# Two waves of an attention and MLP kernel: token order in the copies of x, and one store per output block

## The chip, the cores and the metric

The kernel runs on one core of a Trainium2 chip. The metric is the device time of one execution in microseconds (us); lower is better. Engines are called as the profile does: PE is TensorE (PEld its weight loads), DVE is VectorE, ACT is ScalarE, POOL is GpSimd, SP is SyncE, which here only issues DMAs. A q behind the name (SPq) is the engine's own instruction queue.

## The reference

Inputs are q, k and v of 4 batches, 8 heads, 768 positions and 64 dimensions, a decay `lam` per head, and two weights. A causal attention with decay runs in blocks of 64 positions with a state that is carried on; its output is turned into 3072 tokens of 512 channels, and an MLP follows:

```python
intra = np.einsum('bhic,bhjc->bhij', qb, kb) * Dmask[None]
intra = np.einsum('bhij,bhjd->bhid', intra, vb)
inter = np.einsum('bhid,bhde->bhie', qb * lam_pow[None], kv_state)
out[:, :, sl] = intra + inter
kv_state = lam_block[None, :, None, None] * kv_state + np.einsum('bhsd,bhse->bhde', kb_dec, vb)
...
h = x @ w_in                                  # 512 -> 2048
g = h * (1.0 / (1.0 + np.exp(-1.702 * h)))    # GELU, sigmoid form
return (g @ w_out).astype(np.float32)         # 2048 -> 512
```

Every token's output depends on its own x alone in the MLP, so tokens may stand in any order there as long as the store puts them back.

## The kernel before, in words

The work goes in six waves of 512 tokens. Waves 0 and 1 (`w < ND`) take the first 256 positions of two batches each: batch 2w+c for c = 0, 1. Waves 2 to 5 take 128 positions of all four batches. Within a wave the attention part makes xT[w], a bf16 tile of 128 partitions (channels) by 4 rows r of 512 columns (tokens). `mlp1`, `mlp1_half` and `in_product` then multiply it by w_in, GELU goes to g_sb, and `product0` (wave 0) and `product` (the others) multiply g_sb by w_out. The two products are made mostly by a seven-product scheme on halves: PE works on halves of 256 tokens and of the channels, and DVE forms the sums (`x_sums`, `g_sums`, `weight_sums`).

**Order of tokens in the first two waves.** q, k and v are loaded with `"h (s a) d -> s h (a d)", a=2`: partition s holds positions 2s and 2s+1. So the attention output of 128 positions comes out of PE with its 128 columns as (a s): first the 64 even positions, then the 64 odd ones. `d_x` (L328) copies such a PSUM bank `[128, 4, 128]` into 128 adjacent columns of each of the four rows of xT. It is called four times a wave, for c = 0, 1 and i = 0, 1, with columns from (2c+i)*128: five of the eight copies go to ACT (L224, `act_copy`), three to DVE (L221, `dve_copy`): the last of each `end(w, c)`. All columns of the MLP keep the order (a s), and so does the output block: partition p = 64a+s holds position 2s+a. Stores undo it: each block of 128 partitions by 2x256 f32 is stored in two transfers of 64 partitions (`A` and `Z`) into every second row of out, by `store` in `leave0` (L537, wave 0, kept in `late` and issued later by hand) and by `after_product` (L492, wave 1). Waves 2 to 5 store 128 partitions at once (L496).

**Order of the work.** Instructions stand on each engine's queue in the order in which the kernel is written (`manual_schedule`); a layer beneath puts the waits in, from what each instruction reads and writes. The places that matter:

- Wave 0, its last copies: `end(0, 1)` (L765), with `d_x` for i = 0 on ACT and i = 1 on DVE. Then three `mlp1_half` (L767): the first on the columns of c = 0, the next two on c = 1; then `mlp1` for 12 pieces of w_in, `in_sums`, `sums` and `weight_sums` on DVE, and `product0`.
- Wave 1: `end(1, 0)` (L822), `mlp1_half(1, 0, 14, 15)`, more attention, `a1 b1 a2` (`in_product` on columns of c = 0), `end(1, 1)` (L837), `x_sums(1, (0,))`, then "b2" (L839, `in_product` n = 2: rows 2 and 3 of xT, columns of c = 0), then `mlp1_half(1, 1, 14, 15)` (L842) on columns of c = 1.
- SP's queue: loads of wave 2, `late[2]`, `late[5]` (L846), transposes of wave 2 by DMA (L248), loads of v, `late[3]`, `late[4]`, loads of wave 3, the stores of wave 1, the transposes of wave 3, and so on. A DMA takes one of eight semaphores in turn.

Of the kernel before, what the change touches and what calls it, by code (L numbers as in the profile page):

```python
# [25 lines left out]
def kernel(  # L26
# [13 lines left out]
    nc = tc.nc  # L40
    f32 = mybir.dt.float32
    bf16 = mybir.dt.bfloat16
    B, H, S, D = q.shape
    P = 128
# [70 lines left out]
    A, Z = slice(0, 64), slice(64, P)  # L115
# [78 lines left out]
    cast, trans, masked, xT, g_of, h_ps, o_ps, t_ps = {}, {}, {}, {}, {}, {}, {}, {}  # L194
# [132 lines left out]

    def d_x(w, c, i, t, copy):  # L328
        n0 = (2 * c + i) * P
        copy(xT[w][:, :, n0 : n0 + P], t)  # L330

    def n_scores(w, p):
        s2 = [acc("ps_s") for _ in range(2)]
# [117 lines left out]
    def product(w, n, ts):  # L451
        last = w == NW - 1
        key = ts[0] if last else 0
        if n == 1 and (last or ts[0] == 0):
            for c in "QVX":
                blocks[w, c, key] = acc(f"ps_{c}", shape=[P, 2, 256], tag="a" if last and ts[0] else "mm")
        bank = blocks[w, CHAIN[n], key]
        sums, raw = half_sum.get(w, [None] * 4), [[token_half(w, i, kh) for kh in range(2)] for i in range(2)]
        x = {1: raw[0][0], 2: raw[0][1], 4: raw[1][1], 5: sums[0], 6: sums[1], 7: sums[2], 3: sums[3]}[n]
        for t in ts:  # L460
            for m in range(FFC // 2):
                y = {1: (0, 0), 2: (1, 0), 3: (1, 1)}.get(n)
                y = w_half(m, *y) if y else TS[{4: 3, 5: 0, 6: 1, 7: 2}[n]][:, m]
                nc.tensor.matmul(bank[:, t], x[:, m, t * P : (t + 1) * P], y,  # L464
                                 start=(n in (1, 2, 7) and t == ts[0] * last and m == 0),
                                 stop=(m == FFC // 2 - 1), skip_group_check=True)
        if last or ts[-1] == 1:
            t = slice(ts[0], ts[0] + 1) if last else slice(0, 2)
            if n == 2 and 0 < w < NW - 1:
                c11[w] = partial(after_product, w, n, bank, t)  # L470
            else:
                after_product(w, n, bank, t)

    def after_product(w, n, bank, t):
        if n in (1, 6, 7):
            part[w, n, t.start] = op.tile([P, 2, 256], f32, tag="part", bufs=6, name="part")
            nc.scalar.copy(part[w, n, t.start][:, t], bank[:, t])
            if (w, 4, t.start) in c12:
                after_product(w, 4, c12.pop((w, 4, t.start)), t)
            return  # L480
        if n == 4 and (w, 6, t.start) not in part:
            c12[w, 4, t.start] = bank
            return
        o = op.tile([P, 2, 256], f32, tag="o", name="o_sb")
        if n == 3:
            nc.scalar.copy(o[:, t], bank[:, t])
        else:
            nc.vector.tensor_tensor(o[:, t], part[w, {2: 1, 5: 7, 4: 6}[n], t.start][:, t], bank[:, t], op=ADD)
        i, c = {2: (0, 0), 3: (0, 1), 4: (1, 0), 5: (1, 1)}[n]
        cols = slice(256 * c, 256 * c + 256)  # L490
        if w < ND:
            rows5 = out.rearrange("(b t s a) d -> a b s t d", t=S // P, s=64, a=2)  # L492
            for a, rows in enumerate((A, Z)):
                nc.sync.dma_start(out=rows5[a, 2 * w + i, :, 0:2, cols], in_=o[rows])
        else:
            nc.sync.dma_start(  # L496
                out=out.rearrange("(b s) d -> s b d", s=S)[w * P : (w + 1) * P, 2 * i + t.start : 2 * i + t.stop, cols],
                in_=o[:, t])
# [19 lines left out]
    def leave0(n):  # L518
        bank = blocks[0, BANK0[int(n)]]
        if n in (1, 6, 7):  # L520
            part[0, n] = op.tile([P, 2, 256], f32, tag="part", bufs=6, name="part")
            nc.scalar.copy(part[0, n], bank)
            return
        if n == 4.5:
            nc.gpsimd.tensor_tensor(o21[0], o21[0], part[0, 7], op=ADD)
            return
        o = op.tile([P, 2, 256], f32, tag="o", name="o_sb")
        if n == 3:
            nc.scalar.copy(o, bank)
        else:  # L530
            nc.vector.tensor_tensor(o, part[0, {2: 1, 5: 7, 4: 6}[n]], bank, op=ADD)
        if n == 4:
            o21.append(o)
        i, c = {2: (0, 0), 3: (0, 1), 4: (1, 0), 5: (1, 1)}[n]

        def store():
            rows5 = out.rearrange("(b t s a) d -> a b s t d", t=S // P, s=64, a=2)  # L537
            for a, rows in enumerate((A, Z)):
                nc.sync.dma_start(out=rows5[a, i, :, 0:2, 256 * c : 256 * c + 256], in_=o[rows])
        late[n] = store  # L540

    GR = {w: (1, 2, 0, 3) if w > 1 else (1, 2, 3) for w in range(1, NW)}
# [144 lines left out]
    with tc.manual_schedule():  # L687
# [31 lines left out]
        do_cast(0, 1, "q", nc.vector, 0)  # L719
        do_cast(0, 1, "q", nc.vector, 1)  # L720
        d_x(0, 0, 0, oa, act_copy)
        turn_pe(0, 1, "q", act_copy, 0)
        d_inter(0, 0, oz, 0, False)
        turn_pe(0, 1, "k", dve_copy, 1)
        turn_pe(0, 1, "q", dve_copy, 1)
        d_x(0, 0, 1, oz, act_copy)
        fill(1, "a")
        d_scores(0, 1, 0, True)
# [19 lines left out]
        def end(w, c):  # L748
            oa, oz = d_out(w, c)
            t = acc("ps_kv", shape=[P, NP, D]) if w else states[w, c]  # L750
            if w == 0:
                nc.scalar.copy(seen, oz[:, 3, P - 1 : P])
            d_state(w, c, t, Z)
            if w == 0:
                d_inter(w, c, oz, 0, False)
            d_x(w, c, 0, oa, act_copy)
            d_x(w, c, 1, oz, dve_copy)
            if w == 0:
                nc.scalar.copy(kv_sb[0][:, 2 * w + c], t)
            return partial(nc.vector.tensor_tensor, kv_sb[0][:, 2 * w + c], kept.get((w, c)), t, op=ADD)  # L760
# [131 lines left out]
```

## Time and profile before

| what | value |
|---|---|
| runs | 193.22 us median of 3 (192.25, 193.22, 193.78) |
| profiled execution | 193.47 us, its span 191.8 us |
| granted clock of PE | 1.0 |
| copies into xT, waves 0 and 1 | 5 on ACT, mean 591 ns; 3 on DVE, mean 691 ns |
| copies into xT, later waves (L397) | 16 on ACT, mean 600 ns |
| stores of 64 partitions, 128 KB (L494, L539) | 16, issue 605 and 606 ns of SP (median) |
| stores of 128 partitions, 256 KB (L496) | 12 |
| DMA traffic | 33.91 MB, 177 GB/s over the span |

The span goes from the first to the last instruction that the profile shows; the execution's time is 1.67 us longer. A line of the timeline has the start in us, the length in us, the engine, the line of the kernel, the operation, the tile written and those read, and how many such instructions are merged; in square brackets stands the idle time before it and what ended it. A group's line ends with the sum of busy time in us, the mean of one in ns, and the idle time ahead of the group's instructions. Matmuls are pipelined: one may be shown as 272 ns while the next starts 109 ns later.

### The profile page before, as it was taken

The page shows a single profiled execution, that of the slowest core. Times are in us where ns is not written, and L with a number is a line of the kernel's source. Part 1 is how long each engine was busy: PE and PEld are TensorE (multiplying, and loading weights), DVE is VectorE, ACT ScalarE, POOL GpSimd, SP SyncE. Part 2 cuts the span into 40 slices and gives each one's busy share as a digit, 9 for nine tenths or more (in the row PEclk, how much of TensorE's full clock was granted, in tenths as well). Part 3 has the DMA queues.
Part 4 walks back from the last instruction along what each step waited for, and adds up shares of the span by engine and source line. Part 5 has one row for each costly group of instructions (what it writes and reads, how often), then busy time and mean ns, then how long its engine had stood idle before and what let it go on. Part 6 is the DMA issues. An engine that isn't in the chain of part 4 may idle for free.

```text
span 191.8 us, 5553 instructions
## 1 busy us (share of the span) xinstructions
PE 183.5 (96%) x2291; PEld 150.7 (79%) x2293; DVE 154.6 (81%) x296; ACT 130.0 (68%) x243; POOL 53.8 (28%) x79
## 2 busy tenths in 40 slices
PE   7779999999999999999999999999999999999993
PEld 2356545898788888888888888888888888888882
DVE  1797689997687899979799879799889797889950
ACT  4858566055869976389878388877388876597711
POOL 5298200029738000096000294000393000000000
PEclk9999999999999999999999999999999999999999
DMA  5999999999996799988899756999365903300113
GB/s 154 322 241 161 199 206 206 277 291 295 258 174 139 162 228 243 241 206 135 190 244 221 228 137 140 226 249 251 104 163 121 208 4 113 109 3 0 53 57 112
DMA packets 89599, 33.91 MB, mean 177 GB/s; under 512 B 67430, under 2 KB 89446, under 8 KB 89574
## 3 DMA queue, kind: packets, MB, share of 16 engines
q1 hardware_dynamic: 84676, 28.84, 61.7%
q0 software_dynamic: 4896, 4.72, 14.9%
q8 instruction: 18, 0.29, 0.7%
q14 instruction: 7, 0.06, 0.1%
q10 hardware_dynamic: 2, 0.00, 0.0%
HBM read 27.26 MB, written 6.29 MB: 175 GB/s over the span
## 4 chain that ended last, share of the span: by engine, by line
PE 79%; DMA 12%; DVE 4%; POOL 2%; SPq 1%; issue 0%; ACT 0%; ACTq 0%
PE ps_X L464 19%; PE ps_hX L596 17%; PE ps_V L464 9%; PE ps_hV L596 9%; DMA w_out<-in_moe_w_out_dram 6%; DMA vf<-in_v_dram 6%; PE ps_Q L464 5%; PE ps_hQ L596 4%; PE ps_X L514 3%; DVE w_out_t L431 2%; PE ps_s L338 2%; PE ps_o L393 2%; PE ps_h L417 2%; DVE g_s L444 2%; POOL w_in L184 1%; PE ps_o L380 1%
## 5 line engine op out<-in xcount | busy, mean ns | idle before, releaser
L615 ACT ACTIVATE g_sb<-h_sb 128x512 bf16<-128x512 f32 x57 | 34.5, 632 | 1.2 <-DVE h_sb L604 1.2
L464 PEld LDWEIGHTS <-g_s 128*128 128x128 bf16 x320 | 30.9, 98 | 4.1
L596 PEld LDWEIGHTS <-w_in_t 128*128 128x128 bf16 x304 | 29.7, 98 | 3.6
L224 ACT COPY part<-ps_hX 128x512 f32<-128x512 f32 x34 | 19.5, 586 | 10.4 <-PE ps_hX L596 10.3
L464 PEld LDWEIGHTS <-g_sb 128*128 128x128 bf16 x240 | 22.8, 98 | 3.4
L596 PEld LDWEIGHTS <-w_in 128*128 128x128 bf16 x228 | 22.1, 98 | 2.8
L596 PE MATMUL ps_hX<-x_s,w_in_t 128*128 128x256 bf16 x152 | 22.5, 272 | 0.0
L444 DVE TENSOR_TENSOR g_s<-g_sb 128x1024 bf16<-128x1024 bf16 (+1 forms) x26 | 16.5, 646 | 5.5 <-ACT g_sb L615 5.5
L464 PE MATMUL ps_X<-w_out_t,g_s 128*128 128x256 bf16 x160 | 19.1, 273 | 0.0
L682 POOL CAST behind_q<-x_s 1x1 f32<-1x1 bf16 x4 | 0.7, 174 | 62.2 <-DVE x_s L577 62.2
L212 POOL TENSOR_TENSOR qs<-qf,q_pow 128x512 bf16<-128x512 f32 x16 | 16.3, 1040 | 0.9 <-PE ps_o L301 0.9
L212 POOL TENSOR_TENSOR ks<-kf,k_pow 128x512 bf16<-128x512 f32 x16 | 16.3, 1039 | 0.1
L604 DVE TENSOR_TENSOR h_sb<-part,ps_hX 128x512 f32<-128x512 f32 x19 | 12.9, 681 | 3.9 <-PE ps_hX L596 3.9
L221 DVE COPY part<-ps_hV 128x512 f32<-128x512 f32 x18 | 12.4, 687 | 3.2 <-PE ps_hV L596 3.2
L604 DVE TENSOR_TENSOR h_sb<-part,ps_hV 128x512 f32<-128x512 f32 x19 | 13.0, 684 | 1.0 <-PE ps_hV L596 1.0
L604 DVE TENSOR_TENSOR h_sb<-part,ps_hQ 128x512 f32<-128x512 f32 x19 | 12.9, 681 | 0.4 <-PE ps_hQ L596 0.4
L615 ACT ACTIVATE g_sb<-ps_hX 128x512 bf16<-128x512 f32 x19 | 11.1, 588 | 1.9 <-PE ps_hX L596 1.9
L347 ACT ACTIVATE sm<-ps_s,inv_pow 128x512 bf16<-128x512 f32 x16 | 10.2, 691 | 2.5 <-PE ps_s L338 2.5
L224 ACT CAST v_sb<-vf 128x1024 bf16<-128x1024 f32 (+1 forms) x12 | 10.4, 906 | 1.6 <-DMA vf<-in_v_dram 1.6
L596 PE MATMUL ps_hQ<-xT,w_in 128*128 128x256 bf16 x76 | 11.4, 273 | 0.0
L596 PE MATMUL ps_hV<-x_s,w_in_t 128*128 128x256 bf16 x76 | 11.4, 273 | 0.0
L596 PE MATMUL ps_hV<-xT,w_in_t 128*128 128x256 bf16 x76 | 11.4, 273 | 0.0
(128 smaller groups left out, 364.4 us busy)
## 6 DMA issues: line engine op xcount, KB each, us to landing
kf<-in_k_dram SPq DMA_DIRECT2D x10, 512.0 KB, 6.3
qf<-in_q_dram SPq DMA_DIRECT2D x10, 512.0 KB, 6.7
vf<-in_v_dram SPq DMA_DIRECT2D x10, 512.0 KB, 5.9
out_dram<-o_sb SPq DMA_DIRECT2D x24, 128.0 KB, 2.4
out_dram<-o_sb SPq DMA_DIRECT2D x12, 256.0 KB, 2.6
w_out<-in_moe_w_out_dram POOLq DMA_DIRECT2D x4, 512.0 KB, 14.8
kf<-in_k_dram SPq DMA_DIRECT2D x4, 256.0 KB, 3.1
qf<-in_q_dram SPq DMA_DIRECT2D x4, 256.0 KB, 4.6
```

The costliest lines, as they stand in the source:

```text
L212: eng.tensor_tensor(x.rearrange("p b (r i j d) -> p j (b r) i d", i=2, j=2, d=D)[:, j], f.rearrange("p h (a d) -> p (h a) d", a=2).rearran ...
L221: nc.vector.tensor_copy(out, in_)
L224: nc.scalar.copy(out, in_)
L338: nc.tensor.matmul(s2[h][:, b, :], kT[hs, (b % 2) * NP + p, :], qT[hs, (b % 2) * NP + p, :], start=True, stop=True)
L347: nc.scalar.activation(sm, s, COPY, scale=inv_pow[:, n : n + 1])
L393: nc.tensor.matmul(ps_o[cs, b, :], vt[:, b, 2 * p + i, :], masked[w, 2 * R + i, j][:, b, :], start=False, stop=True, skip_group_check=True)
L444: nc.vector.tensor_tensor(o, x, y, op=f)
L464: nc.tensor.matmul(bank[:, t], x[:, m, t * P : (t + 1) * P], y, start=(n in (1, 2, 7) and t == ts[0] * last and m == 0), stop=(m == FFC // ...
L514: nc.tensor.matmul(bank[:, t], x[:, m, t * P : (t + 1) * P], y, start=(n in (1, 2, 7, 4) and t == 0 and m == 0), stop=(m == FFC // 2 - 1), ...
L596: nc.tensor.matmul(bank[:, u], z[:, kc], y[:, kc], start=(n in (1, 2, 7) and u + kc == 0), stop=(kc == 1), skip_group_check=True)
L604: nc.vector.tensor_tensor(h, h_part[w, g, {2: 1, 5: 7, 4: 6}[n]], bank, op=ADD)
L615: nc.scalar.activation(g_of[w][:, a : b + 1 : b - a, 256 * i : 256 * i + 256], bank, GELU)
```

## The change

In `d_x` the copy writes with a step of two elements: the columns of PSUM, (a s), go to columns (s a) of xT, so that tokens stand in natural order from there on. Each output block of waves 0 and 1 then holds 128 successive positions, and one transfer of 128 partitions stores it.

```diff
     def d_x(w, c, i, t, copy):
         n0 = (2 * c + i) * P
-        copy(xT[w][:, :, n0 : n0 + P], t)
+        copy(xT[w][:, :, n0 : n0 + P].rearrange("p r (s a) -> p r a s", a=2), t.rearrange("p r (a s) -> p r a s", a=2))
...
         if w < ND:
-            rows5 = out.rearrange("(b t s a) d -> a b s t d", t=S // P, s=64, a=2)
-            for a, rows in enumerate((A, Z)):
-                nc.sync.dma_start(out=rows5[a, 2 * w + i, :, 0:2, cols], in_=o[rows])
+            nc.sync.dma_start(out=out.rearrange("(b t s) d -> b s t d", t=S // P, s=P)[2 * w + i, :, 0:2, cols], in_=o)
...
         def store():
-            rows5 = out.rearrange("(b t s a) d -> a b s t d", t=S // P, s=64, a=2)
-            for a, rows in enumerate((A, Z)):
-                nc.sync.dma_start(out=rows5[a, i, :, 0:2, 256 * c : 256 * c + 256], in_=o[rows])
+            nc.sync.dma_start(out=out.rearrange("(b t s) d -> b s t d", t=S // P, s=P)[i, :, 0:2, 256 * c : 256 * c + 256], in_=o)
```

Lines behind L492 have numbers two lower in the changed kernel, those behind L537 four lower.

## The prediction

> **What bounds the kernel now.** I read the page's busy shares first, then the chain that ended last, then the timeline round the eight copies, and last what each engine waited for.
>
> ```profile
> PE 183.5 (96%) x2291; PEld 150.7 (79%) x2293; DVE 154.6 (81%) x296; ACT 130.0 (68%) x243; POOL 53.8 (28%) x79
> ...
> PE 79%; DMA 12%; DVE 4%; POOL 2%; SPq 1%; issue 0%; ACT 0%; ACTq 0%
> ```
>
> TensorE holds the chain for 79% of the span. In order of time that chain is a DMA of w_out until 29.07 us, vector work (L431, L444) until 37.20, and from 37.24 to 188.6 TensorE alone. So what makes TensorE later after 37.24 is paid in full, and what makes it later before can be lost in its waits for DMA and for L431. The share of the page is too coarse for a change of this size; the two stretches with the last copies of each wave decide. First the timeline of wave 0:
>
> ```profile
> 18.50 2.79 PE L417 MATMUL ps_h<-xT,w_in 128*128 128x256 bf16 x24
> 18.56 0.69 DVE L221 CAST xT<-ps_o 128x512 bf16<-128x512 f32 x1 [1.37 <-PE ps_o L301]
> ...
> 21.14 1.03 PE L405 MATMUL ps_h<-xT,w_in 128*128 128x512 bf16 x3
> ...
> 22.51 9.67 PE L405 MATMUL ps_h<-xT,w_in 128*128 128x512 bf16 x44 [0.35 <-DMA w_in<-in_moe_w_in_dram]
> ...
> 36.38 0.60 PE L514 MATMUL ps_V<-w_out_t,g_s 128*128 128x256 bf16 x4
> ...
> 37.24 0.60 PE L514 MATMUL ps_W<-w_out_t,g_sb 128*128 128x256 bf16 x4 [0.26 <-DVE w_out_t L431]
> ```
>
> The reader is to see that L417 starts at 18.50 while VectorE's copy of the wave's last 128 tokens still runs until 19.25, and that TensorE later waits twice, for w_in (22.51) and for L431 (37.24). The same place in wave 1:
>
> ```profile
> 54.35 0.69 DVE L221 CAST xT<-ps_o 128x512 bf16<-128x512 f32 x1
> 54.49 0.61 PE L596 MATMUL ps_hQ<-xT,w_in 128*128 128x256 bf16 x4
> 55.01 1.37 SPq L248 DMA_TRANSPOSE kT<-ks  x1
> 55.09 0.77 PEld L417 LDWEIGHTS <-w_in 128*128 128x128 bf16 x8 [0.27 <-DVE xT L221]
> 55.10 1.05 PE L417 MATMUL ps_h<-xT,w_in 128*128 128x256 bf16 x8
> ```
>
> Four matmuls of L596 run beside the copy, and L417 waits for its end (55.04). They fill TensorE's wait.
>
> **Part 1: the waits of TensorE.** In the built program no instruction of PE, DVE, ACT or POOL is added, removed or moved. Two waits of PE move, and no other wait between compute engines does. In both waves the wait for the last x copies (VectorE's and ScalarE's) stood ahead of the first matmul on the second 256 tokens; now it stands ahead of one that reads only the first 256. In wave 0 it moves from the first matmul of the c=1 half at L767 to the second one of the c=0 half: the first of that half reads row 0 of xT, columns 0 to 255, which lie ahead of the written ones, and does not wait. In wave 1 it moves from the half at L842 to the four matmuls of "b2" (L839). It looks as if the layer that sets waits takes a strided write as one stretch from its first to its last element, rows between included.
>
> *Wave 1.* "b2" starts after the copy, at 55.09 and not at 54.49, and L417 behind it. Eight matmuls of 128x256 start 0.87 us apart (32.02 to 32.89, L514), so one takes 0.109 us and four 0.44. L417 starts at 55.53, not 55.10: **+0.44 us**. Queued behind it on TensorE is everything up to 188.6, a chain of TensorE alone, and VectorE's L604 of "b2" comes later with it. So nothing covers this.
>
> *Wave 0.* The second matmul of L417 starts at about 19.30 (copy's end 19.25, plus the 0.05 that L417 took after 55.04), not at 18.61: 0.69 us late. The 24 matmuls and four of L405 follow. Those take (9.67-0.38)/43 = 0.216 us each, so the fifth of L405 could start at 21.14+0.69+0.87 = 22.70; its weights come at 22.51. That leaves 0.19. At 37.24 TensorE waits for L431: four matmuls from 36.38 are done feeding at 36.82, so there is 0.42 of slack, provided that L431 isn't late. It isn't: the sums L444 that need the GELUs start at 26.15, 30.69 and 33.87, and the GELUs end at 25.91, 29.37 and 32.82; only the first could slip, by under 0.1, and VectorE idles 0.21 before 29.10. **0 us**, and 0.69 with both covers gone.
>
> **Part 2: the copies.** Eight copies (five ACT, three DVE, L224 and L221) write bf16 at a step of 4 bytes, read PSUM as before, and have runs of 64. Their rows and the nearest ones, from the groups with forms apart:
>
> ```profile
> L224 ACT CAST xT<-ps_o 128x512 bf16<-128x512 f32 x5 | 3.0, 591 | 0.4 <-PE ps_o L319 0.4
> ...
> L221 DVE CAST xT<-ps_o 128x512 bf16<-128x512 f32 x3 | 2.1, 691 | 2.2 <-PE ps_o L301 2.2
> ...
> L156 ACT ACTIVATE kd_pow<-ln_lam,i_kd 128x8 f32<-128x8 f32 x2 | 0.5, 294 | 0.1
> L156 ACT ACTIVATE qd_pow<-ln_lam,i_qd 128x8 f32<-128x8 f32 x2 | 0.5, 287 | 0.0
> ...
> L689 ACT ACTIVATE k_pow<-ln_lam,i_k 128x16 f32<-128x16 f32 x1 | 0.3, 293 | 0.0
> ```
>
> Lower end, zero: the same engines write 512 f32 elements, 4 bytes from one to the next, in 586 (L224, part<-ps_hX) and 687 ns (L221, part<-ps_hV), so a pitch of 4 bytes costs nothing when dense, and width costs nothing. Runs of 64 are free too: L205's take 420 ns for 256 elements, L488's dense ones 418 to 421. A gain is excluded, since no copy of 512 out of f32 PSUM is under 578. Upper end: the only writes with gaps are L156's, into every second element. Dense k_pow takes 293 for 16 elements, and at (586-372)/256 = 0.84 ns an element 8 should take 286; qd_pow takes 287, kd_pow 294. So a gap costs 0 to 1 ns an element, 0 to 0.5 us a copy; on VectorE a doubled rate is 0.53, from 687 less 420. I take zero, by the copies, which are nearest in size and engine; 0.53 stays for the range.
>
> [...]
>
> With a price d a copy: wave 0 gives d-0.23 (0.19+d against 0.42). In wave 1, VectorE's copy 48.38 to 49.07 has 0.26 before L417 at 49.38: d-0.26. At 54.35 it is d in full. For d = 0.53 the whole is 0.30+0.27+0.44+0.53 = 1.54.
>
> **Part 3: the stores.** Sixteen stores of 128 KB become eight of 256. SP spends 0.6 us on an issue (L539 606, L494 605 ns, medians), so its queue gains some 4.8 us: four issues ahead of wave 2's transposes and loads, four ahead of wave 3's. Bytes and pieces of 1 KB stay; the 256 KB stores of later waves land in 2.6 us, the halves in 2.4. I count it at zero: from 50 us on, before which no moved store is issued, no compute engine shows a wait for a DMA. Wave 2's last transpose waits for POOL's cast until 62.1 in any case. TensorE's weight loads at the first scores that use the transposes (L338, 66.35) show 0.2 us of plain issue, as in every later wave.
>
> **Sum.** The profiled run took 193.47 us, 191.8 of span and 1.67 round it; 193.47+0.44 = **193.9**. It lies 0.25 over the median of the runs shown, 193.22 (192.25 to 193.78). That spread, 0.8%, is why a measurement of this kernel can tell about 1% from no change.
>
> **Rivals.**
> 1. *Absorbed or not felt*: a slack that the trace hides takes up the 0.44. For it: the run spread is larger than 0.44. Against it: 150 us of chain with TensorE alone. 193.4.
> 2. *The strided write costs* (slower). VectorE's and ScalarE's copies take twice the time per element, by the kd_pow row; VectorE's last copy of wave 1 is the place, since TensorE waits for it twice over. Price 1.54: 195.0. Over 1% (1.93 us) it comes only from d = 0.66 on (3d-0.05), past both engines' doubled rate. For it: kd_pow. Against it: qd_pow, and the f32 copies.
> 3. *SP's queue was a hidden bound* (faster): earlier transposes and loads speed up waves 2 and 3. What it can give is bounded by the 0.2 us of issue at L338 in each of two waves, and it loses the 0.44 all the same; to end 1% faster it needs a wait for a DMA that the view of waits doesn't have. 193.5, at most 0.4 below the forecast.
> That the change doesn't do what it says is out: the built program has eight fewer issues on SP and eight copies that write 4x2x64.
>
> **Chances.** Forecast 0.58, absorbed 0.16, strided write 0.21, SP's queue 0.05. A little under a fifth is past +1%: the part of rival 2 where d passes 0.66, and surprises in the new waits such as wave 0's covers gone (0.69) on top of a price d. Of rival 3 and run spread 0.05 is past -1%. Faster 0.05, same 0.77, slower 0.18. The range goes from 192.6 (absorbed, 193.4, less 0.8 for runs as far apart as 192.25 and 193.22) to 195.2 (rival 2's 195.0 and a little of that spread).
>
> **What would show it.** In the profile after: "b2" of L596 (L592 there) starts behind VectorE's copy near 55.1 and L417 near 55.5; the three halves of wave 0 start near 19.3, but TensorE's wait at 37.2 shrinks to about 0.2 and the time there stays. The eight copies stay at 591 and 691 ns; SP's transposes of wave 2 begin near 52. The copies' mean decides rival 2 at once: from 1.2 us on VectorE it has its price. A later start at 37.24, or one at 66.35 that isn't later by 0.44, would make the steps wrong.

## The result and the profile after

The changed kernel takes 193.43 us in the median of 22 runs, the kernel before 192.73 in as many beside them: a ratio of 1.0038, 95% interval 1.0022 to 1.0055, or 0.73 us (0.42 to 1.06) slower. The forecast was +0.44 and 193.9 us, in a range of 192.6 to 195.2. Its base of 193.47 us was one execution, 0.74 above the median that the kernel before has here.

The profiled execution took 194.43 us, its span 192.7. It is one in which the granted clock of TensorE was 0.79 from 10 to 18 us, while 17 of the 22 runs of this kernel had a mean of 1.0; wave 0's first eight matmuls of L417 take 1.40 us in it, against 1.05 before. So this execution is 0.67 us late at the last L301 (18.83 against 18.16), ahead of anything that the change does. Of that, 0.40 was there when L417 started, at 15.88; how much of the 0.40 is the clock stays open, since in the other traces of the table below L417 starts between 14.88 and 15.59. Behind 18 us the clock was 1.00, and from there on the two traces can be set beside each other. The chain of the page:

```profile
PE 93%; DVE 4%; ACT 1%; issue 1%; DVEq 0%; ACTq 0%
```

Before it had 12% of DMA (w_out and v) and TensorE from 37.24 us alone; now TensorE holds the chain almost from the start. By itself this shows no loss: of two kernels further down whose waits stand as before, one has 93% of TensorE and no DMA too (e2_blocks), the other 79% and 11% of DMA (e8_blocks_read). The timeline round wave 0's last copies (start, length, engine, line, operation, count, idle time before and what ended it):

```profile
18.83 0.30 PE L301 MATMUL ps_o<-qT,kv 64*64 64x128 bf16 x4
...
19.06 0.28 PE L417 MATMUL ps_h<-xT,w_in 128*128 128x256 bf16 x1
19.24 0.73 DVE L221 CAST xT<-ps_o 128x512 bf16<-128x512 f32 x1 [1.58 <-PE ps_o L301]
...
20.02 2.69 PE L417 MATMUL ps_h<-xT,w_in 128*128 128x256 bf16 x23 [0.68 <-DVE xT L221]
...
22.54 1.67 PE L405 MATMUL ps_h<-xT,w_in 128*128 128x512 bf16 x7
```

One matmul of L417 runs, and 23 wait 0.68 us for VectorE's copy, as forecast. But L405 then goes on without a wait for w_in: before, its fifth matmul had waited 0.35 us. And in wave 1:

```profile
54.82 0.73 DVE L221 CAST xT<-ps_o 128x512 bf16<-128x512 f32 x1
...
55.60 0.61 PE L592 MATMUL ps_hQ<-xT,w_in 128*128 128x256 bf16 x4 [0.57 <-DVE xT L221]
55.65 0.42 DVE L573 TENSOR_TENSOR x_s<-xT 128x512 bf16<-128x512 bf16 x1
55.94 0.86 PEld L417 LDWEIGHTS <-w_in 128*128 128x128 bf16 x8
56.05 1.04 PE L417 MATMUL ps_h<-xT,w_in 128*128 128x256 bf16 x8
```

"b2" (L592 here) now stands behind the copy, and L417 behind "b2". The copies, from the groups with forms apart (sum of busy us, mean ns, idle before):

```profile
L224 ACT CAST xT<-ps_o 128x512 bf16<-128x512 f32 x5 | 3.7, 737 | 0.4 <-PE ps_o L319 0.4
...
L221 DVE CAST xT<-ps_o 128x512 bf16<-128x512 f32 x3 | 2.2, 728 | 1.9 <-PE ps_o L301 1.9
```

ScalarE's went from 591 to 737 ns, VectorE's from 691 to 728. SP's queue, round the first moved stores:

```profile
49.73 3.60 SPq L535 DMA_DIRECT2D out_dram<-o_sb  x2
53.43 1.40 SPq L248 DMA_TRANSPOSE kT<-ks  x1
```

The first transpose of wave 2 came 1.6 us earlier than before's 55.01, and TensorE gained nothing by it (stretch B of the table below is 138.73 us here, and 138.74 with the stores in two again).

**How the traces are compared.** A time of this kernel moves by a per cent from one execution to the next (the kernel before took 192.13 to 193.78 us in its 22 runs), but two stretches of a trace tell more than its length. Stretch A goes from the start of wave 0's first L417 to the start of wave 1's last L262 (before: 15.48 to 50.36); the copies and the moved wait of wave 0 are in it. Stretch B goes from there to the start of the last copy of o_sb (ACT, L486; before: 188.62); wave 1's moved wait and nearly all that is left of the program are in it. All traces, the experiments' too, in us:

| kernel | waits early in wave | copies | stores per block | A | B |
|---|---|---|---|---|---|
| before | none | dense | two | 34.88 | 138.26 |
| e5_before_again | none | dense | two | 34.27 | 138.27 |
| changed | 0 and 1 | strided | one | 34.95 | 138.73 |
| e1_waits | 0 and 1 | dense | two | 34.93 | 138.71 |
| e2_blocks | none | strided | one | 33.97 | 138.31 |
| e3_two_stores | 0 and 1 | strided | two | 35.00 | 138.74 |
| e6_wave1_wait | 1 | dense | two | 34.11 | 138.70 |
| e7_wave0_wait | 0 | dense | two | 34.74 | 138.26 |
| e8_blocks_read | none | dense, PSUM read woven | one | 34.15 | 138.28 |

B takes two values, 138.26 to 138.31 and 138.70 to 138.74, and the early wait of wave 1 alone decides which. A is 34.74 to 35.00 with the early wait of wave 0, and anything from 33.97 to 34.88 without. (In the changed kernel's 34.95 the lower clock has a part of about 0.27 us: its last L301 starts 2.95 us behind the first L417, before's 2.68.)

### The profile page after: what moved, and what is told of

It reads as the page before. It is cut to its first block, busy times and chain, and to the rows that moved or that the text cites. A ratio compares the mean times of both kernels' runs of the same rounds, so it can differ in the third digit from the quotient of the medians.

```text
span 192.7 us, 5542 instructions
## 1 busy us (share of the span) xinstructions
PE 184.9 (96%) x2293; PEld 152.0 (79%) x2293; DVE 155.1 (80%) x296; ACT 130.6 (68%) x243; POOL 54.3 (28%) x79
## 4 chain that ended last, share of the span: by engine, by line
PE 93%; DVE 4%; ACT 1%; issue 1%; DVEq 0%; ACTq 0%
PE ps_X L464 18%; PE ps_hX L592 17%; PE ps_V L464 9%; PE ps_hV L592 9%; PE ps_h L405 5%; PE ps_Q L464 5%; PE ps_hQ L592 4%; PE ps_h L417 4%; PE ps_X L512 4%; PE ps_s L338 2%; PE ps_fill L147 2%; PE ps_t L241 2%; PE ps_o L393 2%; DVE qs L205 1%; DVE sm L270 1%; PE ps_s L262 1%
## 5 line engine op out<-in xcount | busy, mean ns | idle before, releaser
L592 PEld LDWEIGHTS <-w_in_t 128*128 128x128 bf16 x304 | 29.7, 98 | 3.6
L592 PEld LDWEIGHTS <-w_in 128*128 128x128 bf16 x228 | 22.1, 98 | 3.4 <-DVE xT L221 0.7
L592 PE MATMUL ps_hX<-x_s,w_in_t 128*128 128x256 bf16 x152 | 22.5, 272 | 0.0
L592 PE MATMUL ps_hQ<-xT,w_in 128*128 128x256 bf16 x76 | 11.4, 273 | 0.6 <-DVE xT L221 0.6
L592 PE MATMUL ps_hV<-x_s,w_in_t 128*128 128x256 bf16 x76 | 11.4, 273 | 0.0
L592 PE MATMUL ps_hV<-xT,w_in_t 128*128 128x256 bf16 x76 | 11.4, 273 | 0.0
L592 PE MATMUL ps_hX<-x_s,w_in 128*128 128x256 bf16 x76 | 11.4, 273 | 0.0
```

Source lines behind the costliest of these rows:

```text
L592: nc.tensor.matmul(bank[:, u], z[:, kc], y[:, kc], start=(n in (1, 2, 7) and u + kc == 0), stop=(kc == 1), skip_group_check=True)
```

## The experiments

### The waits alone: e1_waits, e6_wave1_wait, e7_wave0_wait

The kernel before, with dense copies and two stores. `mlp1_half` gets a hook behind its first matmul, so that TensorE waits for the copies of the second 256 tokens as early as in the changed kernel, in both waves (e1), in wave 1 alone (e6) or in wave 0 alone (e7).

```diff
-def mlp1_half(w, c, a, b):
+def mlp1_half(w, c, a, b, between=None):
...
+                if between and u + kc == 0:
+                    between()
...
-        for c, a in ((0, 2), (1, 0), (1, 2)):
-            mlp1_half(0, c, a, a + 1)
+        mlp1_half(0, 1, 0, 1, partial(mlp1_half, 0, 0, 2, 3))   # e1 and e7
+        mlp1_half(0, 1, 2, 3)
...
-        one_step(1, "b2")
+        mlp1_half(1, 1, 14, 15, partial(one_step, 1, "b2"))      # e1 and e6
         state()
         x_sums(1, (1, 2, 3))
-        mlp1_half(1, 1, 14, 15)
```

> The kernel before with its dense copies and its two stores per block; only the two waits of TensorE stand as early as in the changed kernel: in wave 0 and in wave 1 the first matmul on the second 256 tokens is put ahead of the matmuls on the first 256 that stood in front of it. The changed kernel is 0.73 us (ratio 1.0038) slower than before. Theory A, the moved waits make the loss: +0.44 us here, and more, up to +0.7, if wave 0's wait isn't absorbed; b2 starts behind the copy's end near 55.2. Theory B, the slower copies make it (ACT's are 737 ns in place of 591): at most +0.1 us here.

> The kernel before with dense copies and two stores; only wave 1's wait stands early (the first matmul of the second half ahead of b2). From the start of wave 1's last L262 to the last copy of o_sb (ACT L486) 138.70 us, against 138.26 in the kernel before: +0.44, and the same in the time: +0.3 to +0.6 us.

> The kernel before with dense copies and two stores; only wave 0's wait stands early (the first matmul on c=1 ahead of the first half). Theory A0, covered by the waits for w_in and L431: the time of before within 0.15 us, as the prediction had it. Theory A1, covered only where w_in is late: +0.2 to +0.5 us in the median, up to 0.9 where TensorE doesn't wait for w_in. The stretch from wave 1's last L262 to the end stays at 138.26.

Measured: e1 1.0047 (1.0017 to 1.0077), e6 1.0022 (0.9992 to 1.0052), e7 1.0047 (1.0017 to 1.0076). So the waits, without strided copies and without merged stores, cost what the change costs within the noise, and the one of wave 0, priced at nothing, costs something by itself. In microseconds e1 and e7 are some 0.9 above the kernel before, more than the 0.7 (e1) and, in the median, the 0.5 (e7) that were expected at most; between the executions with a mean granted clock of 0.997 or more the medians are 0.4 (e1) and 0.6 us (e7) apart. The times don't tell 0.4 from 0.9 us, and e6's don't tell its loss from none; the stretches do. Wave 1's wait adds 0.44 to B (138.70 against 138.26), the forecast to the hundredth. In e7, B is the old one, and wave 0 reads:

```profile
18.26 0.30 PE L301 MATMUL ps_o<-qT,kv 64*64 64x128 bf16 x4
19.41 2.79 PE L417 MATMUL ps_h<-xT,w_in 128*128 128x256 bf16 x24 [0.85 <-DVE xT L221]
22.04 10.52 PE L405 MATMUL ps_h<-xT,w_in 128*128 128x512 bf16 x48
```

L417 starts 1.15 us behind L301, where e2 and e6, with no wait there, have 0.23, so TensorE is put back by 0.92 us (in the changed kernel by 0.85: the second matmul of L417 starts at 20.02 and not 0.11 behind the first, at 19.17); and behind it L405 runs its 48 matmuls in one piece, with no wait for w_in that could give it back.

### Is the cover always there: e5_before_again

The kernel before, unchanged.

> The kernel before, unchanged, for a second look at its first 40 us. Theory A1: the cover that hides wave 0's wait, TensorE's wait for w_in at the fifth matmul of L405 (0.35 us by the profile) and for L431 at 37.24, isn't there in every execution, since w_in lands at other times. Then this trace may show no wait of TensorE for a DMA of w_in, and from the first L417 (15.48 in the first trace) to the second L262 of wave 1 (50.36) some 34.0 us, not 34.88. Theory A0, the cover is always there: 34.8 to 34.9 again.

Stretch A took 34.27 us, not 34.88, between the two values that were expected of the theories, and nearer to 34.0:

```profile
17.74 0.30 PE L301 MATMUL ps_o<-qT,kv 64*64 64x128 bf16 x4
18.30 2.79 PE L417 MATMUL ps_h<-xT,w_in 128*128 128x256 bf16 x24 [0.25 <-DMA w_in<-in_moe_w_in_dram]
20.93 10.52 PE L405 MATMUL ps_h<-xT,w_in 128*128 128x512 bf16 x48
...
35.65 0.60 PE L514 MATMUL ps_V<-w_out_t,g_s 128*128 128x256 bf16 x4
36.23 0.60 PE L514 MATMUL ps_W<-w_out_t,g_sb 128*128 128x256 bf16 x4
```

This time TensorE waited 0.25 us for w_in at L417, and not at all at L405. In the first trace the wait at L417 was some 0.1 us, and the longer one was at L405. Of the five traces without the early wait of wave 0, only the very first shows the wait at L405 that the prediction had as cover. The other cover, the wait for L431, is in all five, but it was longest in the first: from the four matmuls into ps_V to the next four, into ps_W, 0.86 us pass there (36.38 to 37.24), 0.58 in this trace and 0.50 to 0.70 in the other three, where four matmuls take 0.44. With the early wait it is 0.43 or 0.44 in three traces, no wait, and 0.59 in e3. w_in lands when it lands: its transfers took 9.1 us in the median in the first trace, and 6.9 to 8.5 in the traces of the kernels behind it (7.8 in this one).

### The strided copies with the old waits: e2_blocks

The changed kernel, with xT of the first two waves laid out as two blocks of 256 tokens with four rows each. A write of the second block then reaches over no column of the first, and the built program has all waits between compute engines where the kernel before has them.

```diff
-            xT[w] = xp.tile([P, NP, W], bf16, tag="x", name="xT")
+            xT[w] = xp.tile([P, HF, NP, W // 2], bf16, tag="x", name="xT")    # waves 0 and 1
...
-        n0 = (2 * c + i) * P
-        copy(xT[w][:, :, n0 : n0 + P].rearrange(...), t.rearrange(...))
+        n0 = i * P
+        copy(xT[w][:, c, :, n0 : n0 + P].rearrange(...), t.rearrange(...))
...
-                nc.tensor.matmul(h, w_in_sb[j][:, kc, i * P : (i + 1) * P], xT[w][:, kc, :],
+                nc.tensor.matmul(h, w_in_sb[j][:, kc, i * P : (i + 1) * P], xT[w][:, :, kc, :] if w < ND else xT[w][:, kc, :],
```

`mlp1_half` and `x_half` take their block in the same way.

> The changed kernel, but xT of waves 0 and 1 is laid out block by block of 256 tokens, each block with its four rows, so that a strided write of the second block reaches over no column of the first: all waits of TensorE stand where they stood before. Copies strided, stores merged. Theory A: about the time of before, within 0.15 us (the last copy's 0.04 on DVE stays on the path). Theory B: +0.5 to +0.7 us, with ACT's copies still at 737 ns. Between the two: what is left over before is the copies' share.

Measured: 0.9996 (0.9967 to 1.0025), and B 138.31. The copies are as slow as in the changed kernel:

```profile
L224 ACT CAST xT<-ps_o 128x512 bf16<-128x512 f32 x5 | 3.7, 739 | 0.4 <-PE ps_o L319 0.4
...
L221 DVE CAST xT<-ps_o 128x512 bf16<-128x512 f32 x3 | 2.2, 733 | 2.3 <-PE ps_o L301 2.3
```

So the loss goes with the waits, and the slower copies leave 0.05 us: VectorE's last copy of wave 1, on which TensorE waits directly. ScalarE's 146 ns a copy aren't felt.

### The stores: e3_two_stores

The changed kernel, each block stored in two transfers of 64 partitions again, now of 64 successive tokens.

```diff
-            nc.sync.dma_start(out=out.rearrange("(b t s) d -> b s t d", t=S // P, s=P)[2 * w + i, :, 0:2, cols], in_=o)
+            for rows in (A, Z):
+                nc.sync.dma_start(out=out.rearrange("(b t s) d -> b s t d", t=S // P, s=P)[2 * w + i, rows, 0:2, cols], in_=o[rows])
```

and so in `store`.

> The changed kernel with its natural token order and strided copies, but each block of waves 0 and 1 stored in two transfers of 64 partitions again. If the merged stores are worth nothing, as forecast: the changed kernel's time, +0.73 us over before, within 0.2. Theory C, the merged stores win something that the rest hides: slower than the changed kernel by more than 0.2 us. If merging costs: faster than it.

Measured: 1.0019 (0.9999 to 1.004), 193.36 us in the median, and B 138.74, as in the changed kernel. Eight issues more on SP change nothing that TensorE sees. The time alone, some 0.37 us over the kernel before, lies outside the 0.2 round 0.73 that was expected and would have left this open, since its interval holds both the changed kernel's ratio and, barely, none.

### What a strided write costs: e4_copy_prices

The kernel before, and behind its end copies of one PSUM bank into scratch, three of each kind on each engine.

```diff
+        s4 = src.rearrange("p r (a s) -> p r a s", a=2)
+        s5 = src.rearrange("p r (a s) -> p r s a", a=2)
+        nc.scalar.copy(to(mb, 1), s4)      # L876 bf16 dense; L877, L878, L879: steps of 2, 4, 8 elements
+        nc.scalar.copy(woven(mb), s4)      # L880 as in the changed kernel
+        nc.scalar.copy(mb[:, 0:512].rearrange("p (r s a) -> p r s a", r=4, a=2), s5)   # L881 dense, read woven
+        ...                                # L882 to L887: the same on VectorE
+        nc.scalar.copy(to(mf, 1), s4)      # L890 f32 dense; L891 step 2; L892 woven; L893 to L895 on VectorE
```

> The kernel before, with copies of one PSUM bank of 128x512 f32 added behind its end, three times each on ACT and on DVE: bf16 dense, at steps of 2, 4 and 8 elements in the source's order, bf16 woven as in the changed kernel (step 2, two runs of 64 a row), bf16 dense with the source read woven, f32 dense, f32 at step 2, f32 woven. Its time is longer by these copies and says nothing. If the pitch in bytes sets the price, f32 dense (4 bytes) costs as bf16 dense, bf16 at step 2 too, and the loss comes from the two runs: step 2 in order 591, woven 737 on ACT. If any gap costs, step 2 in order is at 737 as well, and f32 at step 2 shows whether it is the gap or two-byte pieces.

```profile
L879 ACT CAST g_m<-ps_m 128x512 bf16<-128x512 f32 x3 | 7.3, 2419 | 0.1
...
L878 ACT CAST g_m<-ps_m 128x512 bf16<-128x512 f32 x3 | 3.9, 1290 | 0.1
...
L883 DVE CAST g_m<-ps_m 128x512 bf16<-128x512 f32 x3 | 2.2, 726 | 0.1
L886 DVE CAST g_m<-ps_m 128x512 bf16<-128x512 f32 x3 | 2.2, 726 | 0.1
L877 ACT CAST g_m<-ps_m 128x512 bf16<-128x512 f32 x3 | 2.2, 726 | 0.1
L880 ACT CAST g_m<-ps_m 128x512 bf16<-128x512 f32 x3 | 2.2, 726 | 0.1
...
L894 DVE COPY g_f<-ps_m 128x512 f32<-128x512 f32 x3 | 2.1, 692 | 0.1
...
L887 DVE CAST g_m<-ps_m 128x512 bf16<-128x512 f32 x3 | 2.1, 691 | 0.1
...
L891 ACT COPY g_f<-ps_m 128x512 f32<-128x512 f32 x3 | 1.8, 607 | 0.1
...
L876 ACT CAST g_m<-ps_m 128x512 bf16<-128x512 f32 x3 | 1.8, 587 | 13.6 <-DVE g_m L887 13.6
L881 ACT CAST g_m<-ps_m 128x512 bf16<-128x512 f32 x3 | 1.8, 585 | 0.1
```

The two runs of 64 cost nothing (L877 and L880 agree); the gap does, and nearly for bf16 alone. At step 2 both engines take the same 726 ns, which ScalarE feels (587 dense) and VectorE hardly does (691). If 160 ns, which fits these three, are taken as fixed, the rest doubles from step 2 to 4 and from 4 to 8 (726, 1290, 2419; VectorE's L884 and L885 take 1289 and 2419). f32 at step 2, at the same 8 bytes as bf16 at step 4, takes 607 and 692 (585 and 692 dense). So it isn't the pitch in bytes. Reading PSUM woven and writing dense is free (L881 585 ns against 587 dense, L887 691 against 691).

### The change without its losses: e8_blocks_read

e2's layout, and the order turned round on the reading side:

```diff
-        copy(xT[w][:, c, :, n0 : n0 + P].rearrange("p r (s a) -> p r a s", a=2), t.rearrange("p r (a s) -> p r a s", a=2))
+        copy(xT[w][:, c, :, n0 : n0 + P].rearrange("p r (s a) -> p r s a", a=2), t.rearrange("p r (a s) -> p r s a", a=2))
```

> A version with the change's stores and none of its losses: natural order and one store per block, xT of waves 0 and 1 laid out by blocks of 256 tokens, and the copies read PSUM woven and write dense (585 on ACT and 691 ns on DVE in the price list). All waits stand as before. Expected: the time of before or of the version with blocks (ratio 0.9996), within 0.2 us; copies at 591 and 691 ns; stretch from wave 1's last L262 to the end 138.26. If merged stores win something once nothing else is lost, it is faster than before by what they win.

Measured: 0.9995 (0.9957 to 1.0033), B 138.28, copies at 591 and 692 ns. It undoes the loss and wins nothing, so merging the stores is worth nothing here even with all else as before. The layout by blocks is needed in it: with xT as it was, the built program moves the two waits for a copy of this shape too, though it writes one dense stretch in each row (seen in the built program; that version was not run).

## Why the prediction was right, and where it wasn't

**The sign and the cause were right.** The loss is made by the two waits that the strided writes move, not by the copies and not by the stores (e1 against e2 and e3). That 193.9 came within 0.5 us of the measured 193.43 is partly luck: the base was 0.74 too high and the loss 0.29 too small, and the two errors have opposite signs.

**Wave 1, +0.44.** Measured 0.44 to 0.45 in e6 and e1, and 0.47 in the changed kernel with VectorE's slower copy. No cover, as reasoned from the chain.

**Wave 0, 0 us.** This is the term that was wrong. The step "its weights come at 22.51" took one execution's landing of w_in for a fixed time, and the 0.42 of slack at 37.24 hung on w_out in the same way. In the four further traces without the early wait TensorE doesn't wait at L405, and the slack ahead of the matmuls that wait for L431 is 0.06 to 0.26. So the delay of some 0.9 us (the 0.69 of the prediction was counted from a start that already waited 0.1 for w_in) goes through in full or in part. In the changed kernel's trace the matmuls of 37.24 start at 37.71 with no wait left ahead of them, where the prediction had 0.2; that they start later can't be put down to the change alone, with 0.67 of lateness from before it.

A measured 34.89 in the mean of e1, e3 and e7, and 34.28 in the mean of the five without, 0.6 apart, with single traces from none to 1.0; some 0.1 of it is a wait at L319, ahead of the moved one, in e1 and e3. Where the rest comes from shows when all waits of TensorE inside the stretch are taken off A (behind L301 those beyond the 0.23 us that L417 needs in any case): some 33.8 us are left in each of the eight traces with a clock of 1.00 there. The early wait adds 0.82 to 0.92 us. The other waits behind L301 (for w_in, for L431, and for the copies at the old place) make 0.16 to 1.04 us without it and at most 0.15 with it. So the old waits cover a part of the delay, and all of it only in the first trace. By the medians of the times, 0.73 less the 0.47 of wave 1 leaves some 0.26 for it, and e7's times give 0.6 to 0.9. The size isn't settled closer than that: the intervals of the ratios and a handful of traces hold all of these. The prediction had 0.69 for "both covers gone", as a surprise inside a rival; it should have been a case with a chance of its own.

**The copies, zero.** The term was mis-sized: +146 ns on ScalarE, +37 on VectorE, within the 0 to 0.5 kept for the range. The f32 copies, taken as the nearest rows, misled: their pitch is the same, but their pieces are of four bytes with no gap between them (585 ns on ScalarE in e4's L890, against 726 for bf16 at step 2). kd_pow's 7 ns over its neighbours had the right sign by luck: by e4 gaps in f32 cost ScalarE 22 ns for 512 elements, under 1 ns for kd_pow's 8. On the path only VectorE's 37 ns counts, as the places of the prediction had it (0.05 in B of e2).

**The stores, zero.** Right (e3, e8). The place was off: the transposes began at 53.4, not near 52, since two merged issues took SP 3.6 us and not 1.2.

**Rivals.** "Absorbed" is out by B. "The strided write costs" had the right mechanism, though not by the row that it rested on, with a third of its price on ScalarE and less than a tenth on VectorE, where it mattered. "SP's queue" is out by e3.

## What to carry to other kernels

Look at the waits in the built program before pricing an edit of an access pattern: a strided write may be tracked as everything between its first and its last element, and readers of neighbouring columns then wait for it (here 0.68 us in wave 0 and 0.57 in wave 1); a layout that keeps such writes apart brings the old waits back, as in e2. A cover that is a wait for a DMA, or for work that follows one, is worth what it is worth in several executions, not in the one that was profiled: the wait at L405 was 0.35 us in the first trace and absent in the four others with the old waits of wave 0. If an order has to be turned round in a copy out of PSUM, turn it on the reading side: in e4 such a bf16 copy took 585 ns on ScalarE and 691 on VectorE, and 726 on both with the step in the write.

## What the runs showed of the hardware that was not expected

In e4 ScalarE and VectorE copied 512 elements a partition from f32 in PSUM to bf16 with gaps in equal times, which grow with the step: 726 ns at a step of two elements on both, 1290 and 1289 at four, 2419 at eight, against 587 and 691 dense. f32 at a step of two took 607 and 692, against 585 and 692 dense. Reading PSUM at a distance of 64 elements cost nothing on either (585 and 691).
